# An edge-message kernel: steps of 8 tiles as chunks of their own, instead of chunks of 12 tiles that run across steps

## The chip, the cores and the metric

The kernel runs on one core of a Trainium2 chip. The metric is the device time of one execution in microseconds (us). The kernel before takes 8919.56 us, the median of three runs that lie between 8911.16 and 8920.2.

## What is computed

There are N = 12500 nodes with D = 64 features, and E = 800000 edges with 16 features each. The source and the destination of an edge are random.

```python
N, deg, D, De = 12500, 64, 64, max(16, 1)
E = N * deg
...
m_in = jnp.concatenate([x[src], x[dst], e_attr], axis=-1)
msg = _silu(m_in @ w_msg)
agg = _segment_sum(msg, dst, N)
return _silu(jnp.concatenate([x, agg], axis=-1) @ w_upd)
```

Per edge the message is silu(A[src] + B[dst] + e_attr·W), where A = x·W1 and B = x·W2 are computed once per node. The messages are summed over the edges of each destination, and an update per node follows. Everything is float32.

## The kernel before, in words

**Two flows in one loop.** The 800000 edges are 6250 tiles of 128 edges (one edge per partition). Edges come in random order, and the sum over destinations wants them sorted. So the kernel sorts them coarsely into 128 buckets of BK = 98 destination nodes: a *record* is one edge's 16 features and one packed word (source and the destination's place in its bucket), R = 17 floats. The first flow (class `Step`, L379 to L469) takes 8 tiles at a time and moves their records to a store `st` in DRAM, bucket by bucket. The second flow (classes `Group` and `Batch`) reads tiles of 128 records of one bucket back from the store, gathers A[src] for them, adds the rest of the message, and sums over destinations with a one-hot matmul. The function `period` (L715) issues one step's worth of each flow, several steps and batches deep in a pipeline, so its text is the order of every engine's queue.

**A step.** ScalarE makes the one-hot `hf` of each edge's bucket (L396, L397). `sums` (L399) adds up one-hots over the tiles, so that `count` (L418) can get, with matmuls into `z`, for each edge its rank: how many edges of its bucket stand before it in the chunk. VectorE reduces that to `rank` (L433). `expand` (L435) writes, for every edge, a row of *slots* of 17 floats into `X`: the record stands in the slot of its rank, all other slots are zero (L446, two tiles at a time). `move` (L449) multiplies: the matmul of `hf` (128 edges by 128 buckets) with `X` puts each record into its bucket's row and its rank's slot, in the PSUM tile `pl`, and the tiles of a chunk add up there (L463). A tile that comes later in the chunk needs more slots, since more edges of a bucket may stand before it: the limits by position are `LIM`, two tiles each with 13, 17, 21, 24, 27 and 30 slots, so the matmul is 2 + 17·LIM columns wide.

**A chunk.** When the chunk's last tile is in, ScalarE copies `pl` to `blk` (L468). `Chunk.place` (L477) has VectorE look for lost edges (more than the limit, L481) and advance each bucket's write pointer (L482). `Chunk.scatter` (L485) is one indirect DMA, issued by GpSimd, that writes `blk`'s 128 rows to the buckets' pointers in the store. The next chunk's row begins where the last valid record ended, and overwrites the empty slots.

**Which chunks.** The first K8 = 140 chunks are one step of 8 tiles each, with limits up to 24 (`turn` 3). All others are C = 12 tiles, one and a half steps: three steps (`turn` 0, 1, 2) make two chunks. Then the counts of a chunk's first steps have to be carried into the next step: `before` (L414) names the carried sum, `sums` needs additional adds for it (L409, L410), and `count` an additional matmul in places (L428). There are 782 steps, 140 + 428 = 568 chunks, and so 568 scatters. In turn 1 `move` is cut in two: the first four tiles end one chunk, the other four begin the next and come behind `product` on TensorE (L762 to L766).

**A batch.** A batch is up to 8 tiles of the store. GpSimd issues one indirect DMA per tile, the gather of A[src] (L649): 8 per period, four ahead of the scatter of the previous period's chunk and four behind it (L722 to L727). TensorE transposes the one-hots and features (L668), ScalarE copies them from PSUM (L671), TensorE multiplies by B and W (L677), VectorE adds the gathered rows (L681), ScalarE applies silu (L682), TensorE sums by destination (L698) and VectorE adds to `ACC` (L710). Gathers have four buffers, `GB` (L368): the first gather of a batch waits for the sum that read that buffer (L653).

**What sets the order.** All of it is written by hand in `period`; there is no scheduler. A planner on the host (class `Draws`) forms groups only of records that are surely in the store, from the number of tiles already placed (L888 to L890). Groups come in three stages (`FIRST`, L37): units of one tile, then of two tiles with 6 tiles a batch, then of four tiles with 8 a batch. The loads of a group (SP, L569) wait for the last scatter before the group was formed (L575). After the last step, batches go on without steps until the store is empty, and then the update per node follows. If any edge was lost, a slow path (L1067 on) goes over those chunks again.

Of the kernel before, what the change touches and what calls it, by code (L numbers as in the profile page):

```python
# [23 lines left out]
C = 12  # L24
N8 = 140
LIM = [k for k in (13, 17, 21, 24, 27, 30) for _ in range(2)]
S = LIM[-1]
S8 = LIM[M - 1]
# [12 lines left out]
RK = float(C * P)  # L41
# [7 lines left out]
def mpnn_kernel(tc, x, e_attr, src, dst, w_msg, w_upd, out):  # L49
# [4 lines left out]
    assert E % P == 0 and NB <= NBK and NT >= C  # L54
    K8 = min(N8, NT // (2 * M))
    NCH = K8 + (NT - K8 * M + C - 1) // C
    CAPT = (K8 * S8 + (NCH - K8) * S) // P + 2
# [15 lines left out]
    with es:  # L73
# [43 lines left out]
        limc = cp.tile([P, 4, M], F32, name="limc")  # L117
        for k in range(4 * M):
            nc.vector.memset(limc[:, k // M, k % M:k % M + 1], RK + LIM[k % M if k >= 3 * M else k % C])
# [7 lines left out]
        Gs = cb[:, P + M * S:2 * P + M * S]  # L127
        ps1 = cb[:, 2 * P + M * S:2 * P + M * S + 1]
# [104 lines left out]
        T1, GAP = NT - (NT - K8 * M) % C, -(NT - K8 * M) % C  # L233
        T2 = NT + GAP
        T3 = T2 + -T2 % M

        def spread(buf, src, t0, n):

            clip = lambda t: min(n, max(0, t - t0))
            for a, b, o in ((0, T1, 0), (T1, T1 + GAP, None), (T1 + GAP, T2, GAP), (T2, T3, None)):  # L240
                i, j = clip(a), clip(b)
                if i < j and o is None:
                    nc.vector.memset(buf[:, i:j], 0.0 if buf.dtype == F32 else 0)
                elif i < j:
                    nc.sync.dma_start(buf[:, i:j], src[:, t0 + i - o:t0 + j - o])
# [8 lines left out]
        def seg_prep(di, si, n, t0=0):  # L254
            hi = sg.tile([P, SEG], F32, name="shi")
            lo = sg.tile([P, SEG], F32, name="slo")

            floor_ops(hi[:, :n], lo[:, :n], di[:, :n], -HI_SC, -HI_OFF)
            nc.vector.scalar_tensor_tensor(out=lo[:, :n], in0=hi[:, :n], scalar=float(BK), in1=di[:, :n], op0=OP.mult, op1=OP.add)

            for a, b in ((T1, T1 + GAP), (T2, T3)):
                a, b = max(0, a - t0), min(n, b - t0)
                if a < b:
                    nc.vector.memset(hi[:, a:b], -float(2 * P))
            return hi, lo, si
# [39 lines left out]
        def next_step(ic):  # L305
# [14 lines left out]
            return Step(ready[si][0][:, c0:c0 + M], rec_t[e0][:, eo:eo + M, :], ic - K8, min(M, T2 - ic * M))  # L320
# [56 lines left out]
        prior = dict(step=None, pl=None)  # L377

        class Step:  # L379


            def __init__(c, hi, rec, index, n=M):

                c.hi, c.rec, c.n = hi, rec, n
                c.turn = index % 3 if index >= 0 else 3
                c.size = C if index >= 0 else M
                c.pos = [(c.turn * M + k) % C if index >= 0 else k for k in range(M)]
                c.prev, prior["step"] = prior["step"], c

                c.last = {k: K8 + (index * M + k) // c.size for k in range(n) if c.pos[k] == c.size - 1}  # L390
# [8 lines left out]
            def sums(c):  # L399
# [6 lines left out]
                for a in ((0, 1), (1,), (0,), (0,))[c.turn]:  # L406
                    k = c.G[:, a, 2, :]
                    if a == (1 if c.turn == 0 else 0) and c.turn in (0, 2):
                        nc.vector.tensor_tensor(out=Gs, in0=c.before(a), in1=h[:, a, 3, :], op=OP.add)  # L409
                        nc.vector.tensor_tensor(out=c.G[:, a, 3, :], in0=Gs, in1=k, op=OP.add)  # L410
                    else:
                        nc.vector.tensor_tensor(out=c.G[:, a, 3, :], in0=k, in1=h[:, a, 3, :], op=OP.add)

            def before(c, a):  # L414

                return c.G[:, 0, 3, :] if a else c.prev.G[:, 1, 3, :]

            def count(c):  # L418

                hb = c.hf.bitcast(BF16).rearrange("p m (b two) -> p m b two", two=2)[:, :, :, 1]  # L420
                c.z = pz.tile([P, M, NBK], F32, name="z")
                for a in range(2):
                    k = a * ZB
                    first = c.pos[k] == 0
                    nc.tensor.matmul(c.z[:, k:k + ZB, :], w1, hb[:, k:k + ZB, :], start=True, stop=False)
                    nc.tensor.matmul(c.z[:, k + 1:k + ZB, :], onesb, c.G[:, a, 0:ZB - 1, :], start=False, stop=first)  # L426
                    if not first:
                        nc.tensor.matmul(c.z[:, k:k + ZB, :], onesb, c.before(a)[:, None, :].to_broadcast([P, ZB, NBK]), start=False, stop=True)  # L428
# [6 lines left out]
            def expand(c, rs=None):  # L435
# [6 lines left out]
                nc.vector.tensor_tensor(out=c.x[:, :, 1], in0=rank, in1=limc[:, c.turn, :], op=OP.is_ge)  # L442
                nc.vector.tensor_tensor(out=hit, in0=ioS[:, None, :].to_broadcast([P, M, S]), in1=rank[:, :, None].to_broadcast([P, M, S]), op=OP.is_equal)
                for k in range(0, c.n, 2):
                    n = LIM[c.pos[k]]
# [3 lines left out]
            def move(c, part=None):  # L449

                end = None
                whole = c.turn == 3

                for k in reversed(range(c.n)) if whole else range(c.n):
                    n = c.pos[k]
                    if part is not None and part != (c.turn == 1 and k >= C - M):
                        continue
                    if n == (c.size - 1 if whole else 0):
                        prior["pl"] = pp.tile([P, 512], F32, name="pl")
                    pl = prior["pl"]  # L460
                    w = 2 + LIM[n] * R
                    ends = n == (0 if whole else c.size - 1)
                    nc.tensor.matmul(pl[:, 0:w], c.hf[:, k, :], c.x[:, k, 0:w], start=(n == (c.size - 1 if whole else 0)), stop=ends, skip_group_check=True)  # L463
                    if ends:
                        w = 2 + LIM[c.size - 1] * R
                        end = Chunk(*c.last.values())
                        end.blk = bp.tile([NBK, XR], F32, name="blk")[:, 0:w]
                        nc.scalar.activation(end.blk, pl[:, 0:w], AF.Copy)  # L468
                return end  # L469

        class Chunk:


            def __init__(c, index):
                c.index, c.m = index, M if index < K8 else min(C, NT - K8 * M - (index - K8) * C)
# [239 lines left out]
        def period(step=None, batch=None, ptr_new=None):  # L715
# [154 lines left out]
        def step():  # L870
# [5 lines left out]
            if pipe["z"] and pipe["z"].last:  # L876
# [11 lines left out]
            if pipe["z"]:  # L888
                for i in pipe["z"].last.values():
                    draws.place(Chunk(i).m)  # L890
# [176 lines left out]
        with tc.If(more > 0):  # L1067
# [4 lines left out]
            with tc.If(nover > 0):  # L1072
# [23 lines left out]
                rounds = nc.values_load(fi[0:1, 1:2], min_val=0, max_val=C * P // RS + 1, skip_runtime_bounds_check_because="a count of rounds")  # L1096
# [3 lines left out]
                with tc.For_i(0, nover, 1):  # L1100
# [5 lines left out]
                    w0 = cp.tile([1, 4], F32, name="w0")  # L1106

                    nc.vector.tensor_scalar(out=w0[:, 2:3], in0=f1[:, 2:3], scalar1=-float(K8), scalar2=0.0, op0=OP.add, op1=OP.max)
                    nc.vector.tensor_scalar(out=w0[:, 3:4], in0=f1[:, 2:3], scalar1=float(K8), scalar2=float(C - M), op0=OP.is_ge, op1=OP.mult)
                    nc.vector.tensor_scalar(out=w0[:, 2:3], in0=w0[:, 2:3], scalar1=float(C - M), scalar2=None, op0=OP.mult)  # L1110
                    nc.vector.scalar_tensor_tensor(out=w0[:, 2:3], in0=f1[:, 2:3], scalar=float(M), in1=w0[:, 2:3], op0=OP.mult, op1=OP.add)
                    nc.vector.tensor_scalar(out=w0[:, 0:1], in0=w0[:, 2:3], scalar1=float(NT - C), scalar2=None, op0=OP.min)
                    nc.vector.tensor_tensor(out=w0[:, 1:2], in0=w0[:, 2:3], in1=w0[:, 0:1], op=OP.subtract)
                    nc.vector.tensor_scalar(out=w0[:, 2:3], in0=w0[:, 3:4], scalar1=float(M), scalar2=None, op0=OP.add)
                    nc.vector.tensor_copy(fi[:, 2:3], w0[:, 0:1])
                    bps = pp.tile([P, 512], F32, name="bps", tag="pl")
                    nc.tensor.matmul(bps[:, 0:2], oner, w0[:, 1:3], start=True, stop=True)
                    skip = cp.tile([P, 2], F32, name="skip")
                    nc.vector.tensor_copy(skip, bps[:, 0:2])
                    tv = nc.values_load(fi[0:1, 2:3], engines=(ENG.SP,), min_val=0, max_val=NT - C, skip_runtime_bounds_check_because="the start of a chunk")  # L1120
                    window = lambda buf, src: nc.sync.dma_start(buf, src[:, ds(tv, C)])
                    hi, lo, si = seg_prep(*seg_load(window, C), C, -NT)
                    rec = records(ea_load(window, C), si[:, :C], lo[:, :C], C)
                    off = cp.tile([P, C], F32, name="off")
                    nc.vector.tensor_scalar(out=off, in0=iof[:, 0:C], scalar1=skip[:, 0:1], scalar2=float(2 * P), op0=OP.is_lt, op1=OP.mult)
                    nc.vector.tensor_tensor(out=hi[:, :C], in0=hi[:, :C], in1=off, op=OP.subtract)
# [60 lines left out]
```

## Time and profile before

| | |
|---|---|
| median of three runs | 8919.56 us |
| lowest, highest | 8911.16 us, 8920.2 us |
| span of the profiled execution | 10886.0 us |
| the profile's own total beside that span | none is given: the page has the span from the first to the last instruction alone |
| granted TensorE clock, mean of the span | 0.885 |
| indirect DMAs of GpSimd: gathers, scatters | 6322, 568 |

The span is 22% longer than the median of the runs: this profiled execution was slower than the timed ones. Its durations of single instructions are rows to read; its total isn't the time that is to be predicted. In the profile's page, PE is TensorE's matmuls, PEld its weight loads, DVE VectorE, ACT ScalarE, POOL GpSimd, SP SyncE. A row of a group gives: line, engine, operation, output<-inputs, shape, count | busy us, mean ns of one | idle us of that engine ahead of them, and what ended the idle time. A float32 matmul appears as two records. "issue" is idle time in which the engine waited for nothing that the profile shows; "remote" is a wait that was ended by something that the profile can't name.

### The profile page before, as it was taken

The numbers are of one execution on the slowest core, as the hardware profiler recorded it, in microseconds if no ns is written. First come the engines' busy times: TensorE is split into PE (matmuls) and PEld (weight loads), VectorE is DVE, ScalarE is ACT, GpSimd is POOL, SyncE is SP. The second block draws the span as 40 slices with busy tenths as digits, with TensorE's granted clock in tenths as the row PEclk, the third lists the DMA queues.
The fourth block names the chain that finished last, engine by engine and source line by source line (L and its number), as shares of the span: only waits on it lengthen the run. The fifth ranks groups of instructions, "written<-read, shape, count | busy, mean of one in ns | idle before, by whom it ended". The sixth has DMA issues, their size and how long they took to land. (4 is left out here: it accounts for less than half of the span.)

```text
span 10886.0 us, 155616 instructions
## 1 busy us (share of the span) xinstructions
PE 8949.9 (82%) x49053; PEld 6219.2 (57%) x49816; DVE 7231.4 (66%) x15936; ACT 5082.6 (47%) x12594; POOL 6571.4 (60%) x6908
## 2 busy tenths in 40 slices
PE   8788888888888888888888888888888888888556
PEld 5566655555555555555555555555555555555555
DVE  7777776666666666766666666666666666766232
ACT  6455554444444444444444444444444444544211
POOL 2565666666666666666666666666666666666555
PEclk9999998999989988999998999999899998988555
DMA  3111111111111111111111111111111111111212
GB/s 97 44 49 48 49 49 46 43 47 42 47 42 46 45 44 45 44 43 44 46 43 46 44 44 43 46 47 43 45 42 46 43 47 44 44 45 41 46 36 44
DMA packets 662903, 501.15 MB, mean 46 GB/s; under 512 B 492983, under 2 KB 529911, under 8 KB 662071
## 3 DMA queue, kind: packets, MB, share of 16 engines
q0 software_dynamic: 238976, 349.72, 12.3%
q1 hardware_dynamic: 422775, 141.27, 5.9%
q8 instruction: 400, 6.55, 0.3%
q14 instruction: 432, 3.54, 0.1%
q10 hardware_dynamic: 320, 0.07, 0.0%
HBM read 330.05 MB, written 152.30 MB: 44 GB/s over the span
## 5 line engine op out<-in xcount | busy, mean ns | idle before, releaser
L649 POOL DMA_INDIRECT g<-A_d,sidx x6322 | 5997.6, 949 | 3658.7 <-issue 1620.7
L463 PE MATMUL pl<-X,hf 128*128 128x291 f32 (+5 forms) x12512 | 4745.0, 524 | 476.4 <-issue 428.3
L463 PEld LDWEIGHTS pl<-X,hf 128*128 128x128 f32 x12512 | 2538.7, 211 | 2159.4 <-issue 1737.4
L446 DVE TENSOR_TENSOR X<-cb,rec 128x442 f32<-128x442 f32 (+5 forms) x3128 | 2646.6, 908 | 26.7
L396 ACT ACTIVATE hf<-iof,shi 128x128 f32<-128x128 f32 x6256 | 1908.8, 389 | 1360.4 <-PE pl L463 449.0
L671 ACT ACTIVATE qt<-tq 114x1024 f32<-114x1024 f32 (+1 forms) x818 | 811.7, 992 | 2951.3 <-remote 2298.5
L433 DVE TENSOR_REDUCE rank<-z 128x8 f32<-128x1024 f32 x782 | 954.5, 1221 | 1270.3 <-remote 874.9
L677 PEld LDWEIGHTS pre<-w,qt 114*128 114x128 f32 x10496 | 1392.5, 209 | 687.8 <-ACT qt L671 467.1
L677 PE MATMUL pre<-w,qt 114*128 114x64 f32 x10496 | 1395.2, 291 | 345.6 <-ACT qt L671 317.6
L710 DVE TENSOR_TENSOR ACC<-ag,ACC 64x98 f32 x1938 | 496.7, 256 | 1553.3 <-remote 1131.7
L698 PE MATMUL ag<-q,g 128*64 128x98 f32 x12644 | 882.3, 276 | 490.4 <-remote 236.2
L698 PEld LDWEIGHTS ag<-q,g 128*64 128x64 f32 x12644 | 681.6, 151 | 668.8 <-issue 381.7
L668 PE MATMUL tq<-ident,q 128*114 128x128 f32 x6322 | 929.9, 294 | 103.3 <-issue 91.5
L668 PEld LDWEIGHTS tq<-ident,q 128*114 128x114 f32 x6322 | 812.6, 147 | 238.7 <-issue 122.6
L397 ACT ACTIVATE hf<-hf,ones 128x1024 f32<-128x1024 f32 x782 | 898.8, 1149 | 25.4
L486 POOL DMA_INDIRECT st<-blk,ptrs x567 | 567.2, 1000 | 561.4 <-ACT blk L468 272.2
L659 DVE TENSOR_TENSOR q<-cb,lo 128x784 f32<-128x784 f32 (+1 forms) x818 | 768.7, 940 | 96.1 <-PE ag L698 46.3
L468 ACT ACTIVATE blk<-pl 128x512 f32<-128x512 f32 (+1 forms) x568 | 324.9, 572 | 818.2 <-PE pl L463 500.9
L426 PE MATMUL z<-G,onesb 128*128 128x384 bf16 x1564 | 529.8, 339 | 78.9 <-issue 25.2
L682 ACT ACTIVATE g<-g 128x512 f32<-128x512 f32 (+1 forms) x818 | 498.4, 609 | 192.5 <-DVE g L681 111.8
L681 DVE TENSOR_TENSOR g<-pre,g 128x512 f32<-128x512 f32 (+1 forms) x818 | 541.3, 662 | 51.4 <-issue 37.2
L677 PE MATMUL pre<-BW,qt 114*128 (+1 forms) x2148 | 326.3, 314 | 99.0 <-ACT qt L671 64.8
(138 smaller groups left out, 5243.9 us busy)
## 6 DMA issues: line engine op xcount, KB each, us to landing
g<-A_d,sidx POOLq DMA_INDIRECT x6322
ea<-in_e_attr SPq DMA_DIRECT2D x260, 192.0 KB
rt<-st SPq DMA_DIRECT2D x1312, 34.0 KB
st<-blk,ptrs POOLq DMA_INDIRECT x567
rt<-st SPq DMA_DIRECT2D x434, 8.5 KB
nodes<-in_x SPq DMA_DIRECT2D x62, 98.0 KB
ACC<-rt SPq DMA_DIRECT2D x11, 544.0 KB
rt<-st SPq DMA_DIRECT2D x320, 17.0 KB
```

The costliest lines, as they stand in the source:

```text
L396: nc.scalar.activation(c.hf[:, k, :], iof, AF.Square, bias=c.hi[:, k:k + 1])
L397: nc.scalar.activation(c.hf, c.hf, AF.Relu, bias=ones, scale=-1.0)
L433: nc.vector.tensor_reduce(out=c.rank, in_=c.z, axis=AX.X, op=OP.max)
L446: nc.vector.tensor_tensor(out=c.x[:, k:k + 2, 2:2 + n * R].rearrange("p k (s c) -> p k s c", c=R), in0=hit[:, k:k + 2, 0:n, None].to_broad ...
L463: nc.tensor.matmul(pl[:, 0:w], c.hf[:, k, :], c.x[:, k, 0:w], start=(n == (c.size - 1 if whole else 0)), stop=ends, skip_group_check=True)
L486: i = nc.gpsimd.indirect_dma_start(out=st, out_offset=bass.IndirectOffsetOnAxis(ap=c.ptr, axis=0), in_=c.blk[:, 2:], in_offset=None)
L649: j = nc.gpsimd.indirect_dma_start(out=t.g[:, i, :], out_offset=None, in_=A_d, in_offset=bass.IndirectOffsetOnAxis(ap=t.grp.sidx[:, k:k + ...
L659: nc.vector.tensor_tensor(out=t.q[:, 0:n, 0:BK], in0=ioB[:, None, :].to_broadcast([P, n, BK]), in1=t.grp.lo[:, i0:i0 + n, None].to_broadca ...
L668: nc.tensor.transpose(t.tq[0:KQ, j * P:(j + 1) * P], t.q[:, j, :], ident)
L671: nc.scalar.activation(t.qt[:, 0:w], t.tq[0:KQ, 0:w], AF.Copy)
L677: nc.tensor.matmul(t.pre[:, i * D:(i + 1) * D], t.qt[:, i * P:(i + 1) * P], w, start=True, stop=True)
L698: o = nc.tensor.matmul(t.ag[t.half(v), v // 2 * BK:(v // 2 + 1) * BK], t.g[:, i, :], t.q[:, i, 0:BK], start=(k == 0), stop=(k == u - 1))
```

## The change

Every chunk is one step of 8 tiles. The limits are 13, 17, 21 and 25 slots, two tiles each. Nothing is carried from a step to the next: the adds for the carried counts and the matmul with them across steps are gone, as are the turns, the padding between chunks and the cut in `move`. There are now 782 chunks instead of 568, so 782 evictions `blk`, 782 pointer updates and 782 scatters, one in every step. `move` goes from the last tile to the first, as it did in the 140 first chunks before. The store's room per bucket (`CAPT`) grows from 128 tiles to 154. The slow path for lost edges is simplified accordingly; it isn't shown.

```diff
-C = 12
-N8 = 140
-LIM = [k for k in (13, 17, 21, 24, 27, 30) for _ in range(2)]
+LIM = [k for k in (13, 17, 21, 25) for _ in range(2)]
...
-RK = float(C * P)
+RK = float(M * P)
...
-    K8 = min(N8, NT // (2 * M))
-    NCH = K8 + (NT - K8 * M + C - 1) // C
-    CAPT = (K8 * S8 + (NCH - K8) * S) // P + 2
+    NCH = (NT + M - 1) // M
+    CAPT = NCH * S // P + 2
...
                 for k in (1, 2):
                     nc.vector.tensor_tensor(out=c.G[:, :, k, :], ...)
-                for a in ((0, 1), (1,), (0,), (0,))[c.turn]:
-                    k = c.G[:, a, 2, :]
-                    if a == (1 if c.turn == 0 else 0) and c.turn in (0, 2):
-                        nc.vector.tensor_tensor(out=Gs, in0=c.before(a), in1=h[:, a, 3, :], op=OP.add)
-                        nc.vector.tensor_tensor(out=c.G[:, a, 3, :], in0=Gs, in1=k, op=OP.add)
-                    else:
-                        nc.vector.tensor_tensor(out=c.G[:, a, 3, :], in0=k, in1=h[:, a, 3, :], op=OP.add)
+                nc.vector.tensor_tensor(out=c.G[:, 0, ZB - 1, :], in0=c.G[:, 0, ZB - 2, :], in1=h[:, 0, ZB - 1, :], op=OP.add)
...
                 for a in range(2):
                     k = a * ZB
-                    first = c.pos[k] == 0
                     nc.tensor.matmul(c.z[:, k:k + ZB, :], w1, hb[:, k:k + ZB, :], start=True, stop=False)
-                    nc.tensor.matmul(c.z[:, k + 1:k + ZB, :], onesb, c.G[:, a, 0:ZB - 1, :], start=False, stop=first)
-                    if not first:
-                        nc.tensor.matmul(c.z[:, k:k + ZB, :], onesb, c.before(a)[:, None, :].to_broadcast([P, ZB, NBK]), start=False, stop=True)
+                    nc.tensor.matmul(c.z[:, k + 1:k + ZB, :], onesb, c.G[:, a, 0:ZB - 1, :], start=False, stop=(a == 0))
+                nc.tensor.matmul(c.z[:, ZB:M, :], onesb, c.G[:, 0, ZB - 1, None, :].to_broadcast([P, ZB, NBK]), start=False, stop=True)
...
-            def move(c, part=None):
...
+            def move(c):
+                pl = pp.tile([P, 512], F32, name="pl")
+                for k in reversed(range(c.n)):
+                    w = 2 + LIM[k] * R
+                    nc.tensor.matmul(pl[:, 0:w], c.hf[:, k, :], c.x[:, k, 0:w], start=(k == c.n - 1), stop=(k == 0), skip_group_check=True)
+                end = Chunk(c.index)
+                w = 2 + LIM[c.n - 1] * R
+                end.blk = bp.tile([NBK, XR], F32, name="blk")
+                if w < XR:
+                    nc.vector.memset(end.blk[:, w:XR], 0.0)
+                nc.scalar.activation(end.blk[:, 0:w], pl[:, 0:w], AF.Copy)
                 return end
...
             if p:
-                e = p.move(0)
+                e = p.move()
             if t:
                 t.product()
-            if p:
-                p.move(1)
             if e:
                 e.place(ptr_new)
```

More of the change, by code (lines that the diff above doesn't have):

```diff
@@ L115, in mpnn_kernel @@
         nc.vector.tensor_scalar(out=b98, in0=ipf, scalar1=float(BK), scalar2=None, op0=OP.mult)
-        limc = cp.tile([P, 4, M], F32, name="limc")
-        for k in range(4 * M):
-            nc.vector.memset(limc[:, k // M, k % M:k % M + 1], RK + LIM[k % M if k >= 3 * M else k % C])
+        limc = cp.tile([P, M], F32, name="limc")
+        for k in range(0, M, 2):
+            nc.vector.memset(limc[:, k:k + 2], RK + LIM[k])
         cb = pc.tile([P, 512], F32, name="cb")
@@ L230, in mpnn_kernel @@
         eap = pool("eap", 2)
-        T1, GAP = NT - (NT - K8 * M) % C, -(NT - K8 * M) % C
-        T2 = NT + GAP
-        T3 = T2 + -T2 % M
+        T3 = NCH * M
         def spread(buf, src, t0, n):
[L239 to L245, printed above, removed]
+            k = min(n, NT - t0)
+            if k < n:
+                nc.vector.memset(buf[:, k:n], 0.0 if buf.dtype == F32 else 0)
+            nc.sync.dma_start(buf[:, 0:k], src[:, t0:t0 + k])
         def seg_load(load, n):
@@ L259, in seg_prep @@
             nc.vector.scalar_tensor_tensor(out=lo[:, :n], in0=hi[:, :n], scalar=float(BK), in1=di[:, :n], op0=OP.mult, op1=OP.add)
[L261 to L264, printed above, removed]
+            if NT - t0 < n:
+                nc.vector.memset(hi[:, NT - t0:n], -float(2 * P))
             return hi, lo, si
@@ L375, in mpnn_kernel @@
         live = []
-        prior = dict(step=None, pl=None)
         class Step:
             def __init__(c, hi, rec, index, n=M):
[L384 to L390, printed above, removed]
+                c.hi, c.rec, c.index, c.n = hi, rec, index, n
             def onehot(c):
@@ L441, in expand @@
                 state["x"] = 1 - state["x"]
-                nc.vector.tensor_tensor(out=c.x[:, :, 1], in0=rank, in1=limc[:, c.turn, :], op=OP.is_ge)
+                nc.vector.tensor_tensor(out=c.x[:, :, 1], in0=rank, in1=limc, op=OP.is_ge)
                 nc.vector.tensor_tensor(out=hit, in0=ioS[:, None, :].to_broadcast([P, M, S]), in1=rank[:, :, None].to_broadcast([P, M, S]), op=OP.is_equal)
                 for k in range(0, c.n, 2):
-                    n = LIM[c.pos[k]]
+                    n = LIM[k]
@@ L446, in expand @@
                     nc.vector.tensor_tensor(out=c.x[:, k:k + 2, 2:2 + n * R].rearrange("p k (s c) -> p k s c", c=R), in0=hit[:, k:k + 2, 0:n, None].to_broadcast([P, 2, n, R]),
                                             in1=c.rec[:, k:k + 2, None, :].to_broadcast([P, 2, n, R]), op=OP.mult)
-            def move(c, part=None):
[L451 to L468, printed above, removed]
@@ L474, in __init__ @@
             def __init__(c, index):
-                c.index, c.m = index, M if index < K8 else min(C, NT - K8 * M - (index - K8) * C)
+                c.index, c.m = index, min(M, NT - index * M)
             def place(c, ptr_new):
@@ L875, in step @@
             pn = None
-            if pipe["z"] and pipe["z"].last:
+            if pipe["z"]:
                 if flow["npl"] % 64 == 0:
@@ L888, in step @@
             if pipe["z"]:
-                for i in pipe["z"].last.values():
-                    draws.place(Chunk(i).m)
+                draws.place(Chunk(pipe["z"].index).m)
             period(c, b, pn)
@@ L1111, in mpnn_kernel @@
-                    nc.vector.scalar_tensor_tensor(out=w0[:, 2:3], in0=f1[:, 2:3], scalar=float(M), in1=w0[:, 2:3], op0=OP.mult, op1=OP.add)
-                    nc.vector.tensor_scalar(out=w0[:, 0:1], in0=w0[:, 2:3], scalar1=float(NT - C), scalar2=None, op0=OP.min)
+                    w0 = cp.tile([1, 3], F32, name="w0")
+                    nc.vector.tensor_scalar(out=w0[:, 2:3], in0=f1[:, 2:3], scalar1=float(M), scalar2=None, op0=OP.mult)
+                    nc.vector.tensor_scalar(out=w0[:, 0:1], in0=w0[:, 2:3], scalar1=float(NT - M), scalar2=None, op0=OP.min)
@@ L1119, in mpnn_kernel @@
[L1119 to L1124, printed above, removed]
@@ L1130, in mpnn_kernel @@
-                    halves = [Step(hi[:, 0:M], rec[:, 0:M, :], 0), Step(hi[:, M:2 * M], rec[:, M:2 * M, :], 1, C - M)]
-                    for c in halves:
-                        c.onehot()
-                        c.sums()
-                        c.count()
-                        c.ranks()
-                    def block(rs=None):
-                        for c in halves:
-                            c.expand(rs)
-                            e = c.move()
-                        return e
-                    c = block()
+                    nc.tensor.matmul(bps[:, 0:1], oner, w0[:, 1:2], start=True, stop=True)
@@ new lines, in mpnn_kernel @@
+                    skip = cp.tile([P, 1], F32, name="skip")
+                    nc.vector.tensor_copy(skip, bps[:, 0:1])
+                    tv = nc.values_load(fi[0:1, 2:3], engines=(ENG.SP,), min_val=0, max_val=NT - M, skip_runtime_bounds_check_because="the start of a chunk")
+                    window = lambda buf, src: nc.sync.dma_start(buf, src[:, ds(tv, M)])
+                    hi, lo, si = seg_prep(*seg_load(window, M), M)
+                    rec = records(ea_load(window, M), si[:, :M], lo[:, :M], M)
@@ new lines, in mpnn_kernel @@
+                    off = cp.tile([P, M], F32, name="off")
+                    nc.vector.tensor_scalar(out=off, in0=iof[:, 0:M], scalar1=skip, scalar2=float(2 * P), op0=OP.is_lt, op1=OP.mult)
+                    nc.vector.tensor_tensor(out=hi[:, :M], in0=hi[:, :M], in1=off, op=OP.subtract)
+                    c = Step(hi[:, 0:M], rec[:, 0:M, :], 0)
+                    c.onehot()
+                    c.sums()
+                    c.count()
+                    c.ranks()
+                    def block(rs=None):
+                        c.expand(rs)
+                        return c.move()
@@ L1145, in mpnn_kernel @@
+                    e = block()
                     left = cp.tile([NBK, 3], F32, name="left")
-                    nc.vector.tensor_scalar(out=left[:, 1:2], in0=c.blk[:, 1:2], scalar1=0.0, scalar2=None, op0=OP.is_gt)
-                    nc.vector.tensor_tensor(out=left[:, 0:1], in0=c.blk[:, 0:1], in1=left[:, 1:2], op=OP.mult)
+                    nc.vector.tensor_scalar(out=left[:, 1:2], in0=e.blk[:, 1:2], scalar1=0.0, scalar2=None, op0=OP.is_gt)
+                    nc.vector.tensor_tensor(out=left[:, 0:1], in0=e.blk[:, 0:1], in1=left[:, 1:2], op=OP.mult)
```

30 lines of the change are left out of this document (7 added, 23 removed).

## The prediction, made before the run

> **What bounds the kernel now.** I read the page first (engine totals, then its costliest groups), and compared the span with the timed runs.
>
> ```profile
> span 10886.0 us, 155616 instructions
> PE 8949.9 (82%) x49053; PEld 6219.2 (57%) x49816; DVE 7231.4 (66%) x15936; ACT 5082.6 (47%) x12594; POOL 6571.4 (60%) x6908
> ...
> L649 POOL DMA_INDIRECT g<-A_d,sidx x6322 | 5997.6, 949 | 3658.7 <-issue 1620.7
> ...
> L486 POOL DMA_INDIRECT st<-blk,ptrs x567 | 567.2, 1000 | 561.4 <-ACT blk L468 272.2
> ```
>
> In this execution TensorE (PE) is busiest, with 82%. But the timed runs take 8919.56 us, less than PE's busy sum of 8949.9. So PE's rows can't all hold in the timed runs, and the order of the engines needn't hold either. Part of PE's sum is stretch: the granted clock is 0.885, and 8950 x 0.885 = 7921 us would be left at full clock, an estimate.
>
> The next view is the order of time on POOL alone, in a stretch where it waits for nobody. Columns: start, duration, instruction, idle time ahead of it.
>
> ```profile
> 224.62 0.95 POOL L649 DMA_INDIRECT g<-A_d,sidx  x1 [0.30 <-issue]
> 225.87 0.94 POOL L649 DMA_INDIRECT g<-A_d,sidx  x1 [0.30 <-issue]
> 227.12 0.95 POOL L649 DMA_INDIRECT g<-A_d,sidx  x1 [0.30 <-issue]
> 228.37 1.00 POOL L486 DMA_INDIRECT st<-blk,ptrs  x1 [0.30 <-issue]
> 229.68 0.96 POOL L649 DMA_INDIRECT g<-A_d,sidx  x1 [0.30 <-issue]
> ```
>
> Busy time hides something here: each indirect DMA is followed by 0.30 us in which POOL waits for nothing visible and yet doesn't begin the next one. The pitch is 1.25 us for a gather and 1.30 us for a scatter. The waits between 4000 and 8000 us say that this is the rule (total us, times, longest).
>
> ```profile
> POOL g L649 <- issue: 611.9, 1967, 8.0
> POOL g L649 <- remote: 533.0, 228, 3.6
> ```
>
> 1967 of 2405 gathers have a gap of 611.9 / 1967 = 0.31 us; another 228 wait 2.3 us for something else, so in the profiled execution POOL isn't the last. Now the sum by pitch: 6322 x 1.25 + 568 x 1.30 = 7903 + 738 = 8641 us. That is 79% of the span, but **97% of the timed 8919.56 us**. PE at full clock is 89% of it, DVE's 7231.4 us 81%. By the rows, POOL's pitch is what fits the timed runs and nearly fills them.
>
> Next, rates by step: L433 runs once a step, L649 once a gather (view of windows: stretch, length, busy us, count, clock, DMA share, GB/s).
>
> ```profile
> 5000.00:6000.00 1000.00, 91.58 (x75) 0.91 0.17 45
> ...
> 5000.00:6000.00 1000.00, 571.44 (x603) 0.91 0.17 45
> ```
>
> The first is L433: 75 steps in 1000 us, 13.33 us each. The second is L649: 603 gathers, 8.04 a step. POOL needs 8.04 x 1.25 + 2/3 x 1.30 = 10.92 us a step. The profiled step shrunk by 8919.56 / 10886 is 13.33 x 0.819 = 10.92 us too, an estimate that supposes an even shrinking.
>
> **The change part by part.** Steps 140 to 781, 642 of them, change their form; the first 140 were chunks of 8 tiles already and only go from 24 to 25 slots. Start, tail and update stay.
>
> *POOL, added:* 782 - 568 = 214 scatters. Does a narrower row (425 floats instead of 510) make one cheaper? The same line in two windows, first in the stage of 8-tile chunks (1000 to 1400 us), then of 12-tile chunks (4000 to 8000 us):
>
> ```profile
> L486 POOL DMA_INDIRECT st<-blk,ptrs x36 | 36.0, 1001 | 23.2 <-ACT blk L468 13.2 <-issue 10.0
> L486 POOL DMA_INDIRECT st<-blk,ptrs x200 | 200.2, 1001 | 143.2 <-ACT blk L468 78.4 <-issue 59.4 <-DVE LOST L481 3.9
> ```
>
> 1001 ns in both: it goes by the DMA, not by its width. So 214 x (1.00 + 0.30) = **+278 us** of POOL, 0.43 us a step: 11.35 instead of 10.92. The bounds: +0, if POOL has room for all of it in the timed runs, and 214 x (1.00 + 143.2 / 200) = +368, if every new scatter also brings the mean idle time that stands ahead of scatters here (0.72 us, mostly for `blk`). I take +278, by the free stretch, since an engine that paces the others finds its inputs ready. A Trainium skill page speaks against it: "DMA: Bandwidth & Descriptors", section on the anatomy of one DMA on the SWDGE path, puts dispatch at about 50 ns and descriptor generation as small, so that many can be issued before the cost shows. By that price the 214 scatters would add an estimated 11 us. The 1001 ns of this trace speak against it for indirect DMAs of 128 rows.
>
> *PE, removed:* the view of groups by shape, one row for each width of `move`, and the carried-count matmul:
>
> ```profile
> L463 PE MATMUL pl<-X,hf 128*128 128x410 f32 x2272 | 1030.4, 575 | 90.9 <-issue 76.4 <-DVE X L446 9.3 <-ACT q L660 2.0
> L463 PE MATMUL pl<-X,hf 128*128 128x359 f32 x2272 | 980.0, 547 | 146.3 <-issue 126.8 <-DVE g L681 12.2 <-DVE rank L433 5.9
> L463 PE MATMUL pl<-X,hf 128*128 128x512 f32 x1712 | 821.9, 597 | 28.7 <-issue 25.0 <-DVE slo L259 0.4
> L463 PE MATMUL pl<-X,hf 128*128 128x461 f32 x1712 | 812.5, 589 | 58.5 <-issue 51.5 <-DVE g L681 2.8 <-DVE slo L148 1.1
> L463 PE MATMUL pl<-X,hf 128*128 128x291 f32 x2272 | 780.5, 459 | 114.0 <-issue 112.1
> L463 PE MATMUL pl<-X,hf 128*128 128x223 f32 x2272 | 643.7, 408 | 37.9 <-issue 36.6 <-ACT blk L468 1.2
> L428 PE MATMUL z<-G,onesb 128*128 128x512 bf16 x996 | 393.3, 395 | 1.1 <-DVE X L446 1.1
> ```
>
> Busy time over count is 0.283, 0.344, 0.431, 0.454, 0.475 and 0.480 us a record from 223 to 512 columns. Two tiles of two records each: 4 x 2.467 = 9.87 us per 12 tiles, 6.58 a step. After: 0.283 + 0.344 + 0.431 + 0.460 (427 columns, between 410 and 461), x 4 = 6.07. That is -0.51 us a step, -325 us; the first 140 steps gain 4 x 0.006 us each, +4. L428 falls from 996 to 782, 214 x 0.395 = -85. Sum of PE: **-406 us**, off an engine that I hold to be second.
>
> *DVE, removed and added:*
>
> ```profile
> L446 DVE TENSOR_TENSOR X<-cb,rec 128x816 f32<-128x816 f32 x568 | 566.6, 998 | 0.0
> L446 DVE TENSOR_TENSOR X<-cb,rec 128x1020 f32<-128x1020 f32 x428 | 517.2, 1208 | 0.0
> L446 DVE TENSOR_TENSOR X<-cb,rec 128x714 f32<-128x714 f32 x568 | 508.0, 894 | 7.3
> L446 DVE TENSOR_TENSOR X<-cb,rec 128x918 f32<-128x918 f32 x428 | 475.0, 1110 | 7.3
> L446 DVE TENSOR_TENSOR X<-cb,rec 128x578 f32<-128x578 f32 x568 | 424.9, 748 | 0.0
> L446 DVE TENSOR_TENSOR X<-cb,rec 128x442 f32<-128x442 f32 x568 | 348.4, 613 | 12.2
> L409 DVE TENSOR_TENSOR cb<-G,hf 128x128 f32<-128x128 bf16 x428 | 126.8, 296 | 7.3
> L410 DVE TENSOR_TENSOR G<-cb,G 128x128 bf16<-128x128 f32 x428 | 124.6, 291 | 14.6
> L412 DVE TENSOR_TENSOR G<-G,hf 128x128 bf16<-128x128 bf16 x568 | 174.3, 307 | 19.5
> L482 DVE SCALAR_TENSOR_TENSOR ptrs<-blk,LOST,ptrs 128x1 int32<-128x1 f32 x567 | 125.9, 222 | 20.1
> L481 DVE SCALAR_TENSOR_TENSOR LOST<-blk 128x1 f32<-128x1 f32 x568 | 86.9, 153 | 95.9 <-ACT blk L468 83.3 <-issue 11.8
> ```
>
> The expansion takes 5.571 us per 12 tiles, 3.71 a step; after 0.613 + 0.748 + 0.894 + 1.03 (850 elements) = 3.29, so -0.42 x 642 = -270. The adds: 428 x (0.296 + 0.291) go, 214 x 0.307 come, -185. Two more pointer operations in 214 chunks, +80. DVE: about **-375 us**, beside POOL's work.
>
> *ACT:* 214 evictions more, 782 instead of 568.
>
> ```profile
> L468 ACT ACTIVATE blk<-pl 128x512 f32<-128x512 f32 x428 | 253.6, 592 | 500.2 <-PE pl L463 317.6 <-issue 177.2 <-remote 4.6
> L468 ACT ACTIVATE blk<-pl 128x410 f32<-128x410 f32 x140 | 71.3, 510 | 318.0 <-PE pl L463 183.3 <-issue 96.9 <-remote 30.6
> ```
>
> 782 x 0.524 (427 columns) instead of 325 us: +85 us, hidden in an engine with 53% idle; uncovered it is 0.11 us a step.
>
> *Waits and queues:* the scatter stands in POOL's queue between the fourth and the fifth gather of a batch, and waits for `blk` and the pointer of the period before. Behind it are four gathers; the addition on DVE (L681) waits for them, and DVE's queue behind that. This now happens every step, and costs nothing as long as POOL comes later than ScalarE and VectorE do. `pl` has one buffer and is evicted each step, a period before the next `move`. SP's group loads wait for the last scatter before the group, two periods back. The cut in `move` goes; `product` then waits for all 16 records, up to 8 more than in a third of the steps, on PE, which has the 0.51 us to give. The store's greater room changes addresses only.
>
> **The sum.** The profiled execution is paced by PE's chain (its 228 POOL waits say so), so against its own span I get 10886 - 406 = about 10480: the profile may well become *shorter*. The timed runs stand 18% below that span, where POOL's pitch fills 97%; there PE's and DVE's gains lie beside POOL, and the sum is 8919.56 + 278 = **9198 us** (3.1% slower).
>
> **The rivals.**
>
> *A. PE paces the timed runs too; faster.* If part of the 0.30 us gap belongs to the profiled execution alone, POOL has room and PE's 406 us come off: 8919.56 - 406 = 8514. For it: PE is first in the profile. Against it: the gap of 0.30 us is the same in every stage, and PE's sum exceeds the timed runs. It decides where 9.04 DMAs of pitch p a step fit into 10.92 us: p below 1.20 us, against 1.25 measured. The page named above would have POOL nearly free, and so is on this rival's side.
>
> *B. The two balance.* With p between 1.16 and 1.20, the room taken by the scatters is about what PE gives: 8900 to 8960, no change or slower by a little.
>
> *C. The scatter's inputs come late.* POOL is full and each new scatter also stands idle as the mean one does here: +368, 9288.
>
> *D. Lost edges.* With at most 25 slots for 8 tiles, an edge beyond its limit starts the slow path (L1067). The reference's own `dst`, counted in windows of 8 tiles, has at most 22 edges of one bucket, and none passes its position's limit; so this is nearly out. It would cost more than C.
>
> **How the numbers follow.** Forecast (POOL full, 9100 to 9250): 0.62. A: 0.20. B: 0.07, of it 0.04 no change and 0.03 slower. C: 0.10. D: 0.01. Slower by over 0.2% (about what a measurement of this kernel can tell from no change) is 0.62 + 0.10 + 0.03 + 0.01 = 0.76, within it 0.04, faster 0.20. The range leaves out A but for its weakest form (a gain of up to 60 us) and reaches past C: 8860 to 9300, some 0.8. The likeliest case's own range is 9100 to 9250, since POOL's room before may be up to 0.2 us a step.
>
> **What would show it.** In the profile after: 782 scatters at about 1.00 us and gaps of 0.30 us unchanged; `move` with four widths, 223, 291, 359 and 427; L428's successor x782; DVE near 6860 us, PE near 8540, POOL near 6790 busy. POOL's waits for others ("remote", "PE ag") should shrink towards its pitch of 11.35 us a step, with a span of 10300 to 10700. The forecast is wrong if the timed runs fall, or if POOL's pitch turns out shorter without a profile: then rival A's reading of the 0.30 us holds.

## The result, and the profile after

The changed kernel takes **9205.78 us** (median of 4 runs, 9203.25 to 9207.08), the kernel before 8918.99 us (4 runs): a ratio of 1.0321, 95% interval 1.0307 to 1.0336. It is 287 us slower. The forecast was 9198.

The kernel before takes 8.91 to 8.93 ms in all runs on some chips (the faster kind) and 10.7 to 10.9 ms in all runs on others (the slower kind), so totals of the two kinds aren't compared with each other. The first profile of the kernel before (span 10886.0 us) is of the slower kind by its span; its chip isn't on record. A second profile of the unchanged kernel, the run `before_again` (8909.94 us), is the one to lay beside the profile after.

First the second profile of the kernel before: its page, its windows for L433 (once a step) and L649 (the gathers), and its waits between 4000 and 8000 us.

```profile
span 8908.1 us, 155616 instructions
PE 8177.3 (92%) x49053; PEld 5897.7 (66%) x49816; DVE 7253.4 (81%) x15936; ACT 5059.3 (57%) x12594; POOL 6581.3 (74%) x6908
```

```profile
5000.00:6000.00 1000.00, 111.85 (x92) 0.96 0.23 54
...
5000.00:6000.00 1000.00, 696.06 (x734) 0.96 0.23 54
```

```profile
POOL g L649 <- issue: 719.7, 2362, 0.3
...
POOL st L486 <- issue: 72.8, 239, 0.3
```

Now the same views of the changed kernel (its gathers are L609, its scatters L446, its once-a-step line L401), and POOL alone in order of time.

```profile
span 9205.3 us, 155854 instructions
PE 7782.7 (85%) x48827; PEld 5819.5 (63%) x49590; DVE 6896.9 (75%) x15692; ACT 5092.1 (55%) x12808; POOL 6812.2 (74%) x7122
```

```profile
5000.00:6000.00 1000.00, 106.70 (x88) 0.96 0.24 56
...
5000.00:6000.00 1000.00, 670.48 (x704) 0.96 0.24 56
```

```profile
POOL g L609 <- issue: 689.5, 2262, 0.3
...
ACT blk L428 <- DMA st<-blk,ptrs: 1494.8, 315, 6.9
```

```profile
5021.66 0.95 POOL L609 DMA_INDIRECT g<-A_d,sidx  x1 [0.31 <-DMA g<-A_d,sidx]
5022.91 1.00 POOL L446 DMA_INDIRECT st<-blk,ptrs  x1 [0.30 <-issue]
```

In both, POOL's longest wait in these rows is 0.3 us: from step 140 to step 781 not one gap of more than 0.4 us stands ahead of an indirect DMA, neither before (5537 of them) nor after (5753). POOL's queue is a solid train of 1.25 and 1.30 us wagons, though the page calls it 74% busy. In 1000 us there are 92 steps before and 88 after. The mean step between step 160 and step 780 is 10.90 us before and 11.36 after; steps 140 to 781 make 296 of the 297 us between the two spans. PE, DVE and everything before step 140 or behind the last step do not show in the difference.

The lines of the changed kernel that answer to the prediction's terms, from the groups by shape:

```profile
L609 POOL DMA_INDIRECT g<-A_d,sidx x6322 | 6023.1, 953 | 1949.7 <-issue 1530.6 <-DMA g<-A_d,sidx 244.1 <-DVE ptrs L442 53.9
L422 PE MATMUL pl<-X,hf 128*128 128x427 f32 x3124 | 1352.2, 556 | 565.1 <-ACT blk L428 555.6 <-DVE LOST L441 8.4
L414 DVE TENSOR_TENSOR X<-cb,rec 128x850 f32<-128x850 f32 x781 | 805.3, 1031 | 0.0
L446 POOL DMA_INDIRECT st<-blk,ptrs x781 | 782.4, 1002 | 383.6 <-issue 219.7 <-ACT nodes L191 97.7 <-ACT blk L428 21.2
L428 ACT ACTIVATE blk<-pl 128x427 f32<-128x427 f32 x781 | 411.6, 527 | 3403.9 <-DMA st<-blk,ptrs 2752.5 <-PE pl L422 375.8 <-PE ag L658 198.6
L396 PE MATMUL z<-G,onesb 128*128 128x512 bf16 x782 | 317.3, 406 | 0.0
L386 DVE TENSOR_TENSOR G<-G,hf 128x128 bf16<-128x128 bf16 x782 | 232.3, 297 | 26.9
```

### The profile page after: what moved, and what is told of

Read it like the earlier page. It is cut to its first block, busy times and chain, and to the rows that moved or that the text cites. A ratio compares the mean times of both kernels' runs of the same rounds, so it can differ in the third digit from the quotient of the medians.

```text
span 9205.3 us, 155854 instructions
## 1 busy us (share of the span) xinstructions
PE 7782.7 (85%) x48827; PEld 5819.5 (63%) x49590; DVE 6896.9 (75%) x15692; ACT 5092.1 (55%) x12808; POOL 6812.2 (74%) x7122
## 5 line engine op out<-in xcount | busy, mean ns | idle before, releaser
L609 POOL DMA_INDIRECT g<-A_d,sidx x6322 | 6023.1, 953 | 1949.7 <-issue 1530.6
L422 PE MATMUL pl<-X,hf 128*128 128x427 f32 (+3 forms) x12500 | 3664.8, 446 | 567.7 <-ACT blk L428 558.2
L422 PEld LDWEIGHTS pl<-X,hf 128*128 128x128 f32 x12500 | 2320.1, 190 | 1773.1 <-ACT blk L428 644.6
L414 DVE TENSOR_TENSOR X<-cb,rec 128x442 f32<-128x442 f32 (+3 forms) x3125 | 2376.0, 822 | 26.8
L428 ACT ACTIVATE blk<-pl 128x427 f32<-128x427 f32 x782 | 412.0, 527 | 3409.1 <-DMA st<-blk,ptrs 2757.7
L637 PE MATMUL pre<-w,qt 114*128 114x64 f32 x10496 | 1308.5, 279 | 261.2 <-DVE g L641 143.5
L637 PEld LDWEIGHTS pre<-w,qt 114*128 114x128 f32 x10496 | 1260.2, 195 | 413.0 <-ACT qt L631 371.4
L446 POOL DMA_INDIRECT st<-blk,ptrs x781 | 782.4, 1002 | 383.6 <-issue 219.7
L401 DVE TENSOR_REDUCE rank<-z 128x8 f32<-128x1024 f32 x782 | 948.7, 1213 | 34.6 <-PE z L396 34.6
L658 PE MATMUL ag<-q,g 128*64 128x98 f32 x12644 | 793.6, 268 | 46.7 <-PE tq L628 23.1
L658 PEld LDWEIGHTS ag<-q,g 128*64 128x64 f32 x12644 | 630.6, 147 | 211.9 <-issue 153.9
L441 DVE SCALAR_TENSOR_TENSOR LOST<-blk 128x1 f32<-128x1 f32 x782 | 123.9, 158 | 603.3 <-ACT blk L428 596.9
```

Source lines behind the costliest of these rows:

```text
L401: nc.vector.tensor_reduce(out=c.rank, in_=c.z, axis=AX.X, op=OP.max)
L414: nc.vector.tensor_tensor(out=c.x[:, k:k + 2, 2:2 + n * R].rearrange("p k (s c) -> p k s c", c=R), in0=hit[:, k:k + 2, 0:n, None].to_broad ...
L446: i = nc.gpsimd.indirect_dma_start(out=st, out_offset=bass.IndirectOffsetOnAxis(ap=c.ptr, axis=0), in_=c.blk[:, 2:], in_offset=None)
L609: j = nc.gpsimd.indirect_dma_start(out=t.g[:, i, :], out_offset=None, in_=A_d, in_offset=bass.IndirectOffsetOnAxis(ap=t.grp.sidx[:, k:k + ...
L637: nc.tensor.matmul(t.pre[:, i * D:(i + 1) * D], t.qt[:, i * P:(i + 1) * P], w, start=True, stop=True)
L658: o = nc.tensor.matmul(t.ag[t.half(v), v // 2 * BK:(v // 2 + 1) * BK], t.g[:, i, :], t.q[:, i, 0:BK], start=(k == 0), stop=(k == u - 1))
```

## The experiments

The theory: GpSimd's indirect DMAs pace the timed run, one after the other, and each costs its pitch whatever it moves. Rivals: TensorE paces it (so relief there counts), or the new scatters cost by their waits and buffers.

**The kernel before, profiled again** (no edit), `before_again`.

> The kernel before, unchanged, for a second profile of it. Pitch theory (GpSimd's indirect DMAs pace the timed run: 1.25 us a gather, 1.30 us a scatter): span near 8919 us, POOL's idle time almost all gaps of 0.30 us, its long waits for the reduction and for unnamed events gone, steps of about 10.9 us in the stage of 12-tile chunks, TensorE's clock above 0.885. Rival (TensorE paces the timed run as it did the first profiled one): span near 8919 us, but POOL still waits 2 us once in most steps for the buffer that TensorE's sum must free.

Measured: 8909.94 us (one run), with the rows above. Steps are 10.90 us long, POOL has no long waits, and the granted clock is 0.938. That is the theory's picture, not the rival's.

**More buffers for the chunk**, `after_blk4`. A row above shows a wait that the prediction had not seen: ScalarE's eviction waits 2752.5 us in all for an earlier scatter to land, and TensorE waits for the eviction.

```diff
-        bp = pool("bp", 2)
+        bp = pool("bp", 4)
```

> The changed kernel with four buffers for the evicted chunk instead of two. In its trace ScalarE's eviction waits 1495.6 us between 3000 and 7000 us for an earlier scatter to land, and TensorE waits for the eviction. Pitch theory: that wait lies beside POOL's work, time stays at 9206 us within 10. Rival (the scatter in every step costs time through its buffer: landing, eviction, then TensorE): 100 to 280 us come back, 8920 to 9100.

Measured: 9214.10 us beside 8926.82 of the kernel before on that chip, 1.0321 (1.0304 to 1.0338), the same ratio as without the edit. The eviction's row:

```profile
L428 ACT ACTIVATE blk<-pl 128x427 f32<-128x427 f32 x782 | 402.5, 515 | 689.3 <-PE pl L422 684.8 <-issue 4.3
```

The wait for the landing has gone from 2752.5 us to nothing, and the time hasn't moved: it lies within the theory's 10 us of 9206. It was the wait of an engine that is early, behind one that is late.

**Wider slots**, `after_wide`.

```diff
-LIM = [k for k in (13, 17, 21, 25) for _ in range(2)]
+LIM = [k for k in (16, 21, 25, 28) for _ in range(2)]
```

> The changed kernel with slot limits 16, 21, 25 and 28 (90 a step, where the kernel before had 88 on average and the changed one has 76): TensorE's and VectorE's relief is given back, 782 scatters stay, each of them wider (478 columns). Pitch theory: the relief was worth nothing, 9206 us within 15. Rival (part of the relief was taken, so that POOL's real cost is higher than 278 us): 9250 to 9600.

Measured: 9288.35 us beside 8926.82, 1.0405 (1.0388 to 1.0423): 74 us above `after_blk4` on the same chip. That is outside the theory's 15 us and inside the rival's 9250 to 9600, but not for the rival's reason. The windows by step tell where the 74 us lie; of L401 in the changed kernel first, then in the wide one:

```profile
500.00:1000.00 500.00, 68.06 (x56) 1.00 0.27 62
5000.00:6000.00 1000.00, 106.70 (x88) 0.96 0.24 56
```

```profile
500.00:1000.00 500.00, 63.86 (x53) 1.00 0.25 61
5000.00:6000.00 1000.00, 106.89 (x88) 0.97 0.24 58
```

From step 160 on, the step is 11.36 us in both: there 14 slots more a step are free, and so the relief that the change gave there was worth nothing. All of the loss stands in the first 140 steps (their end is at 1332.7 us instead of 1253.0), where a batch has 6 tiles. The windows of all engines there (PE, PEld, DVE, ACT, POOL), of the changed kernel and then of the wide one:

```profile
500.00:1000.00 500.00, 473.51 (x2907) 351.17 (x2962) 470.77 (x1253) 322.56 (x802) 380.50 (x393) 1.00 0.27 62
```

```profile
500.00:1000.00 500.00, 482.73 (x2716) 328.19 (x2766) 468.06 (x1164) 302.41 (x748) 354.46 (x365) 1.00 0.25 61
```

Between steps 60 and 135 of the changed kernel POOL's DMAs and their gaps fill the step of 8.96 us, without one wait above 0.4 us, and TensorE and VectorE are nearly as full. The slots added 0.79 us of TensorE's busy time and 0.57 us of VectorE's to a step there, steps went to 9.62 us, and POOL now has 68 waits above 0.4 us. So POOL no longer paces that stage. TensorE is then the fullest, with 482.73 of 500 us; whether it or VectorE sets the pace isn't shown. My expectation was wrong by treating the run as one stage; the first 140 steps, with 75 slots each, weren't relieved by the change either.

**Fewer gathers**, `before_6g`, `after_6g`, and both again as `before_6g_b`, `after_6g_b`.

```diff
-                for i in range(lo, min(hi, t.n)):
+                for i in range(lo, min(hi, t.n, 6)):
```

(The gather buffers are also set to zero once.)

> The kernel before with only the first 6 of 8 gathers of a batch (the rows for the other two tiles are left out, so messages of those tiles lack A[src]); everything else is there. GpSimd then needs 6 x 1.25 + 0.87 = 8.4 us a step, TensorE's busy time was 0.937 x 10.9 = 10.2 us a step. Pitch theory: TensorE takes over, steps of 10.3 to 10.7 us, 8350 to 8600 us in all. Rival (GpSimd's DMAs are not what paces it): within 100 us of 8920.

> The changed kernel with the same two gathers a batch left out. GpSimd needs 6 x 1.25 + 1.30 = 8.8 us a step, TensorE's busy time was 0.841 x 11.36 = 9.55 us a step. Pitch theory: with GpSimd out of the way the sign of the change turns round: 7950 to 8250 us, faster than the kernel before with 6 gathers by 3 to 7%. Rival (the scatter in every step costs by its waits, whatever GpSimd's load): the changed form stays slower than the kernel before with 6 gathers, by about 290 us.

> The kernel before with only the first 6 of 8 gathers of a batch (messages of the other two tiles lack A[src]), once more, since the kernel before itself took 10725 us beside the first such run. Pitch theory, where the kernel before takes about 8920 us: TensorE takes over from GpSimd (8.4 us of DMAs a step), steps of 10.2 to 10.6 us, 8350 to 8650 us in all. Rival (GpSimd's DMAs don't pace it): within 100 us of 8920.

> The changed kernel with the same two gathers left out. Pitch theory: with GpSimd out of the way (8.8 us of DMAs a step) the sign turns round, since TensorE has 0.65 us a step less to do: 7950 to 8300 us, 3 to 7% faster than the kernel before with 6 gathers. Rival (the scatter in every step costs by its waits and its buffers, whatever GpSimd's load): slower than the kernel before with 6 gathers by about 290 us.

Measured on one chip: 8921.71 and 9047.69 us, beside 10725.24 of the kernel before; ratios 0.8318 (0.8291 to 0.8345) and 0.8435 (0.8402 to 0.8468). On another chip: 9036.40 and 9172.88 beside 10883.38; 0.8300 (0.8282 to 0.8318) and 0.8425 (0.8406 to 0.8444). The kernel before takes 10.7 to 10.9 ms on these chips, so the totals that I named don't apply, and 8921.71, though near the rival's 8920, says nothing for it. The sign did not turn round there: the changed form stays 1.4 and 1.5% behind (9047.69 / 8921.71, 9172.88 / 9036.40), by 126 and 136 us, which is less than half of the rival's 290. But the size of the fall is telling. 1420 gathers less (4902 instead of 6322) took 1804 and 1847 us off the kernel before, 1.27 and 1.30 us each: the full pitch and a little more, on chips where POOL stood idle about once a batch. The waits of `before_6g_b` between 4000 and 8000 us:

```profile
POOL g L651 <- issue: 582.4, 1879, 5.5
POOL g L651 <- PE ag L700: 520.4, 251, 6.4
```

Between steps 140 and 781 of that trace POOL has 798 waits above 0.4 us, 1656 us in all; with 8 gathers, in the first profile, they are 728 and 1762 us. Without the plain gaps of 0.30 us in them that is 2.2 and 2.4 us a step. If another engine alone set the step, POOL's waits would have grown by the 2.5 us that its train of DMAs lost; they didn't grow. So POOL is on the path there too, beside a stall of about 2 us a step. This is argued and not shown: TensorE stands idle for only 0.6 us of a step in `before_6g_b`, so it may share the path. What makes the stall on these chips stays open. One difference that the traces show is on TensorE: between steps 140 and 781 of the first profile it stands idle 2.1 us a step, 0.62 of it ahead of L463's matmuls with nothing visible that they wait for; in the second profile it is 0.7 us, and none ahead of L463.

**The same on a chip of the faster kind**, `after_6g_c`.

> The changed kernel with two of 8 gathers of a batch left out (messages of those tiles lack A[src]), on a third chip. Where the kernel before takes about 8920 us: POOL's pitch would give 9206 - 1416 x 1.25 = 7440 us if it still paced; TensorE's busy time is 0.841 x 11.36 = 9.55 us a step. Pitch theory: TensorE takes over, steps of 9.6 to 10.2 us, 8000 to 8350 us. Rival (the scatter's waits pace, not GpSimd's DMAs): 9000 us and more. Where the kernel before takes about 10800 us: the fall by about 15% of the two earlier runs comes again, to 9050 to 9200.

Measured: 7624.01 us beside 8909.18 of the kernel before, 0.8557 (0.8533 to 0.8582). Windows of all engines (PE, PEld, DVE, ACT, POOL), of the profile after with all gathers first, then of this run:

```profile
5000.00:6000.00 1000.00, 841.80 (x5366) 622.85 (x5453) 758.88 (x1666) 566.22 (x1438) 758.63 (x792) 0.96 0.24 56
```

```profile
3000.00:4000.00 1000.00, 1000.00 (x6844) 764.47 (x6843) 929.13 (x2090) 704.10 (x1804) 738.58 (x772) 1.00 0.26 63
4000.00:5000.00 1000.00, 1000.00 (x6850) 764.12 (x6849) 927.97 (x2086) 704.24 (x1805) 738.51 (x773) 1.00 0.25 63
```

and POOL's longer waits between 4000 and 8000 us:

```profile
POOL g L611 <- issue: 619.0, 2010, 1.8
POOL st L448 <- ACT blk L430: 123.4, 288, 0.5
POOL g L611 <- DVE g L643: 88.8, 224, 0.7
```

Here TensorE has no idle time at all at full clock, with a step of 9.07 us, and POOL's train (6 x 1.25 + 1.30 = 8.8) now waits a little for the others. So TensorE took over, as the theory has it, but the time is below the 8000 to 8350 us that I named: I had taken TensorE's 0.841 x 11.36 = 9.55 us, busy at a clock of 0.96, for what it needs. The fall from 9205.78 is 1582 us, of the 1775 that the pitch of 1420 gathers alone would give. So in the changed kernel TensorE could go down to 9.07 us a step; POOL's 11.36 hides all of that. Whether the kernel before would then be the slower one on such a chip wasn't tried.

**One more DMA a batch**, `after_extra_half` (64 rows of 256 bytes), once more as `after_extra_half_b`, and `after_extra_thin` (128 rows of 64 bytes).

```diff
+                if hi == BT:
+                    nc.gpsimd.indirect_dma_start(out=SCR[len(gathers) % 4][0:64, :], out_offset=None, in_=A_d, in_offset=bass.IndirectOffsetOnAxis(ap=t.grp.sidx[0:64, t.i0:t.i0 + 1], axis=0))
```

> The changed kernel with one indirect DMA more in each batch, a gather of 64 rows of 256 bytes into a scratch buffer that nobody reads. Pitch by DMA: 818 batches x 1.25 = 1020 us more, 10230 us. Pitch by descriptors (rows): the 0.30 us gap and half of 0.95 us, 818 x 0.78 = 635 us more, 9840 us. Time hidden beside other engines: no change.

> The changed kernel with one indirect DMA more in each batch, a gather of 128 rows of 64 bytes (from the edge features) into a scratch buffer that nobody reads. Pitch by DMA or by rows: 1020 us more, 10230 us. Cost by bytes: a quarter of that, 9460 us.

> The changed kernel with one gather more in each batch, 64 rows of 256 bytes into a scratch buffer that nobody reads. In the first such run this DMA took 906 ns on POOL, against 951 for 128 rows. Pitch theory: 818 x (0.91 + 0.30) = 990 us more than the changed kernel, about 10195 us. Rival (only rows or bytes cost time): 500 us more or less than that, 9700 us at most.

Measured, one run each: 12011.46 and 11998.42 us (half the rows, then thin rows) on the chip with 10725.24, and 12185.36 (half the rows again) on the one with 10883.38, so the totals that I named don't apply. Above the kernel before they are 1286, 1273 and 1302 us. The changed kernel without the extra DMA wasn't run on these chips. Taking off 278 for the change's own scatters, by the forecast's price, leaves 995 to 1024, or 1.22 to 1.25 us for each of 818 DMAs; taking off the 126 and 136 us seen with 6 gathers leaves about 1.4, both of them estimates. Half the rows or a quarter of the bytes make no difference to be seen between the two. The rows of the extra DMA, with half the rows (`after_extra_half_b`) and with thin rows (`after_extra_thin`):

```profile
L617 POOL DMA_INDIRECT scr<-A_d,sidx x818 | 739.1, 904 | 249.3 <-issue 248.7 <-DVE g L644 0.3 <-DVE ACC L673 0.3
```

```profile
L617 POOL DMA_INDIRECT scr<-in_e_attr,sidx x818 | 772.9, 945 | 249.3 <-issue 249.0 <-DVE g L644 0.3
```

They take 904 and 945 ns, with 0.30 us of gap ahead of each. So the price goes by the instruction, and hardly by its rows or bytes.

**The 12-tile form earlier**, `before_n20`.

```diff
-N8 = 140
+N8 = 20
```

> The kernel before with 20 instead of 140 chunks of 8 tiles, so the 12-tile form begins 120 steps earlier, in the stage with batches of 6 tiles: 528 scatters instead of 568. Pitch theory with a place: in that stage GpSimd needs 6.06 gathers and one scatter, 8.95 us a step, and VectorE is busy for 94% of it; the 12-tile form adds about 0.6 us a step to VectorE, which then paces: 40 to 90 us slower, 8960 to 9010. Rival (a scatter costs 1.30 us wherever it stands): 52 us faster, 8867.

Measured: 10923.08 us beside 10883.38, 1.0034 (1.0022 to 1.0046). 40 scatters less and 40 us slower, so taking scatters away doesn't save 1.30 us each wherever they stand. The forecast's mechanism, VectorE pacing that stage, isn't shown by it: on this chip neither POOL nor VectorE is full in that stage (286.99 us of busy time with 300 DMAs, and 413.02, of the 500 us from 500 on). It is inconclusive.

## Why the prediction was right

**The deciding step held:** the pitch, not the busy time, summed over 6890 DMAs and held against the timed runs, not against the span. The 3% that the sum left open were no room for scatters, a point that the prediction had left open with its bound of +0: in `before_again` 201 us lie ahead of the first gather and 21 behind the last, and between them POOL's waits beyond the plain gaps are 35 us in all (34 in the profile after). **The sum of POOL's part** was +278; the timed medians differ by 287, the two spans by 297. 214 x 1.30 is 278 of that, and the gathers' mean grew from 950 to 953 ns, 6322 x 0.003 = 19 more, which I hadn't. That the two add up to 297 exactly is luck: `before_again` ran 17 us below the other runs of this kernel on its chip.

**PE and DVE** gave what was worked out: 8177.3 to 7782.7 is -395 (forecast -406), 7253.4 to 6896.9 is -357 (-375), and the eviction went to 412 us. As forecast, none of it reached the end from step 160 on (`after_wide`). POOL's busy time, 6812, came out near 6790. The wide row of L422, 427 columns, has 1352.2 / 3124 = 0.433 us a record instead of the 0.460 that I took from the first profile.

**What failed: "against its own span I get about 10480", and the sentence ahead of it, that PE's chain paces the profiled execution.** The profile after has 9205.3 us. Two things were wrong. I took the long span for a property of the profiled execution, and by the runs on record it goes with the chip: the same kernel's second profile has 8908.1. And, by the argument above, POOL's waits don't take it off the path on such a chip: with two gathers less a batch, the time fell there by their whole pitch (`before_6g`, `before_6g_b`). PE's forecast of 8540 us busy fell with that span. Whether the change makes the kernel faster or slower on such a chip with all its gathers was not run; with 6 gathers it was 1.4 and 1.5% slower.

**The rivals.** A (TensorE paces) is out: POOL has no room, and the 0.30 us gaps are in every profile. B (the two balance, 8900 to 8960) is out by the time. C (scatters find their inputs late) is out on the faster chips: of 383.6 us idle ahead of L446, 219.7 are plain gaps over 781 scatters, and 97.7 fall behind the node tables. The large wait that the change did add, ScalarE's for the landing of an earlier scatter, was in none of my cases, and costs nothing (`after_blk4`). The rule of the Trainium skill ("DMA: Bandwidth & Descriptors", anatomy of one DMA on the SWDGE path) that many descriptors can be issued before their cost shows agrees with these runs, where 64 rows less save 41 to 47 ns of 950. The Trainium skill's 50 ns of dispatch in the same section do not cover what an indirect DMA costs here, 1.25 to 1.30 us from one start to the next.

## What to carry to other kernels

Sum an in-order queue by its pitch, start to start, in a stretch where it waits for nobody, and hold the sum against the timed runs: an engine that the page calls 74% busy can be full. Relief for another engine is worth nothing as long as that queue has no room, so a form with fewer, wider units can beat one with less work in all. Where a profile's span is far from the timed runs, take a second profile before reading its waits, since an engine that waits can still be on the loop.

## What the runs showed of the hardware

An indirect DMA issued by GpSimd costs nearly the same whatever it moves: 904 ns for 64 rows of 256 bytes, 945 for 128 rows of 64, 950 for 128 of 256, and 1000 to 1007 for scatters of 128 rows of 1632 to 2040 bytes, each followed by 0.30 us before the next begins. TensorE's busy sum isn't a floor: it was 9.55 us a step (0.841 x 11.36, at a granted clock of 0.96) while POOL paced, and 9.07 (at 1.00) when TensorE did. And chips differ by a fifth for this kernel, 8.91 to 8.93 against 10.73 to 10.88 ms, with the same durations of single DMAs (gathers of 949 and 950 ns in the two profiles of the kernel before). Each chip was seen at one time only, and the cause is open.
